# Feature-map attention with a gated MLP on one core: initial loads moved to the sync queue, normalization moved to VectorE

## The chip, the cores and the metric

The kernel runs on one NeuronCore of a Trainium2 chip. The core has a matrix engine (TensorE, PE), three engines for elementwise work (VectorE, DVE; ScalarE, ACT; GpSimd, POOL) and a sync engine (SP) that only issues DMAs. ScalarE and GpSimd can issue DMAs too. Each engine works through its own queue of instructions in order, and engines wait for each other through semaphores. The metric is the device time of one execution in microseconds; lower is better.

## The reference, cut to what matters

There are 8 batches, 8 heads, 576 tokens and a head dimension of 64. Queries and keys are projected to 128 features, and both signs are exponentiated:

```python
def phi(x):
    proj = np.einsum('bhsd,df->bhsf', x, w_phi)
    proj = proj - np.max(np.abs(proj), axis=-1, keepdims=True)
    return np.concatenate([np.exp(proj), np.exp(-proj)], axis=-1)
q_p, k_p = (phi(q), phi(k))
kv = np.einsum('bhsf,bhsd->bhfd', k_p, v)
z = np.sum(k_p, axis=2)
num = np.einsum('bhsf,bhfd->bhsd', q_p, kv)
den = np.einsum('bhsf,bhf->bhs', q_p, z)[..., None] + 1e-06
return (num / den).astype(np.float32)
```

The attention output, as rows of 512 channels, goes through a gated MLP whose gate mixes the tokens of a batch:

```python
h = np.maximum(x @ w_in, 0.0)
u, v = (h[..., :d_ff // 2].copy(), h[..., d_ff // 2:].copy())
mu = np.mean(v, axis=-1, keepdims=True)
var = np.mean((v - mu) ** 2, axis=-1, keepdims=True)
v_n = (v - mu) / np.sqrt(var + 1e-06)
v_s = np.einsum('ts,bsd->btd', w_spatial, v_n) + b_spatial[None, :, None]
gated = u * v_s
return (gated @ w_out).astype(np.float32)
```

## The kernel before

**Tiling.** A batch has 576 = 512 + 64 tokens. The 512 lie on 128 partitions with four tokens each (`main_ap`); the remaining 64, the tail, of two neighbouring batches share one tile of 128 partitions (`tail_ap`, a group g is batches 2g and 2g+1). The list `units` holds the attention work in order: a pair of heads of one batch (`pj` 0 to 3), or the shared tail of a group. Units 0 and 1 are the first two pairs of batch 0, unit 2 the tail of batches 0 and 1, units 3 and 4 the rest of batch 0, units 5 to 8 batch 1, unit 9 the next tail, and so on to 36 units.

**A unit.** `a_transpose` turns tokens and channels of k and q on TensorE (L254, VectorE or ScalarE copies the result, L256); from batch 2 on, `cross` does it with a transposing DMA. `a_keys` projects (L261), takes the largest magnitude per token and head on VectorE (L273, mk) and exponentiates on ScalarE (L276, kf). `a_scale` forms em = exp(-mk) and exp(mk) (L296) and scales v by it on GpSimd: two instructions and a small cast per pair (L301, L303, vs); for a tail `tail_scale` does so on 64 partitions (vst, shown under L61 since `pin` records it). `a_queries` takes the queries' maxima (L287), which go through TensorE and VectorE (`a_max_t`) and are subtracted inside `a_qfeat`: as extra products with `sel` up to batch 1, and from batch 2 on (`merged`) through the combined weights `wm`. `a_kv` sums kf times vs over the tokens (L373), each group of four products closed by one with the tail's vst (L375), so that a first value product needs the tail's scaling. `a_num` and `norm` divide numerator by denominator.

**The MLP of a batch.** When a batch's attention is through, `b_tasks` appends its tasks to a queue: `b_v_tail` and `b_v` (the v half of w_in, L442; ReLU on ScalarE, L444; mean and variance on VectorE, L445 and L446), `b_root`, the four normalizations `b_ln`, the u half (`b_u`, L497), the token mixing `b_s` (L518, with bias and tails in L519), and `b_o` (L543). `root` computes the reciprocal root of the variance by a power on GpSimd and from it a scale and an offset, four small GpSimd instructions (L452 to L455); `normalize` (L459) applies them on GpSimd. The tail's normalized rows go into `vnt`, whose row beside the 64 tail rows holds a one, so that the bias row of `w_spT` is added by the same product.

**Order.** `step(i)` emits the instructions of unit i in the order of `ORDER`, with lags by unit, and lets `fill` interleave MLP tasks by a credit of TensorE time. After each step the entries of `io` for that step are emitted: mostly DMA issues. An instruction wrapped in `pin` keeps its place behind the one written before it on its engine; others may be moved by the scheduler that fixes each queue when the program is built.

**Loads at the start.** SP loads two pairs of heads of batch 0's k and q as fp32 (`first`), then the bias rows (L192, L193), then batch 1's v. GpSimd issues, with the cast to bf16 in the DMA, the tails of k and q, the heads 4 and 5 of k and q, v of batch 0 in two halves, the tail of v and heads 6 and 7; among these it casts half of `first`. A pool of two buffers named v_f holds the v of two batches; k_tl, q_tl and v_tl have one buffer each.

```python
load_tail("k", 0)
load_tail("q", 0)
load("k", 0, 1, 0, 2)
load("q", 0, 1, 0, 2)
load_v(0, 0, nc.gpsimd)
```

Of the kernel before, what the change touches and what calls it, by code (L numbers as in the profile page):

```python
# [16 lines left out]
def kernel(  # L17
# [15 lines left out]
    nc = tc.nc  # L33

    B, H, S, D = q.shape
    F = w_phi.shape[1]
# [3 lines left out]
    P = 128  # L40
# [19 lines left out]
    def pin(start):  # L60
        return lambda *a, **kw: tc.keep_in_program_order(start(*a, **kw))  # L61
# [39 lines left out]
    def load_v(b, y=None, eng=nc.sync):  # L101
        if b not in st:
            alloc(b)
        h0, n = (0, H) if y is None else (4 * y, 4)
        pin(eng.dma_start)(
            out=st[b]["v"][:, h0 * NB:(h0 + n) * NB, :].rearrange("p (h c) d -> p h (c d)", h=n),
            in_=main_ap(v, b, h0, n))

    def load_tail(x, g, veng=nc.sync):
        if g not in gs:  # L110
            alloc_tail(g)
        t, eng = dict(q=(q, nc.gpsimd), k=(k, nc.gpsimd), v=(v, veng))[x]
        for i in range(2):
            pin(eng.dma_start)(out=gs[g][x][i * TL:(i + 1) * TL], in_=tail_ap(t, 2 * g + i))
# [50 lines left out]
    def fill_vnt(i, copy):  # L165
        for bl, row in ((0, TL), (1, 0)):
            pin(copy)(out=vnt[i][:, bl, :], in_=ident[:, row:row + 1].to_broadcast([P, HALF]))

    pin(nc.scalar.copy)(out=vst[0].rearrange("p b s h d -> p (b s h d)"), in_=zero.to_broadcast([P, 4 * H * DA]))
    for y in range(2):  # L170
        r = slice(y * D, (y + 1) * D)
        pin(nc.scalar.copy)(out=wphi2[r, y * F:(y + 1) * F], in_=wphi_f[r, :])
    fill_vnt(0, nc.scalar.copy)
    load_tail("k", 0)
    load_tail("q", 0)
    load("k", 0, 1, 0, 2)
    load("q", 0, 1, 0, 2)
    load_v(0, 0, nc.gpsimd)
    for x in ("k", "q"):
        pin(nc.gpsimd.tensor_copy)(out=half_tile(x, 0, 0)[:, 2:4], in_=first[x, 2])  # L180
    load_tail("v", 0, nc.gpsimd)
    load("k", 0, 1, 2, 2)
    load("q", 0, 1, 2, 2)
    load_v(0, 1, nc.gpsimd)

    w_in_bf = cpool.tile([P, KC, DFF], BF16)
    w_out_bf = cpool.tile([P, KC, DM], BF16)
    wsp = s2.tile([P, NB, T0], BF16, tag="vn", name="wsp", bufs=2)
    wspr = cpool.tile([P, NB, TL], BF16)
    wspt = s2.tile([TL, S], BF16, tag="ob", name="wspt", bufs=6)  # L190
    bsp_row = s2.tile([P, S], FP32, tag="xT", name="bsp_row", bufs=3)
    nc.sync.dma_start(out=bsp_row[TL:TL + 1, :], in_=moe_b_spatial)  # L192
# [11 lines left out]
    def transpose_spatial(i):  # L204

        pt = psum.tile([P, S], BF16, tag="bank", name="pt")
        if i < NB:
            sc = POS[i]
            for tp, c in enumerate(POS):
                nc.tensor.transpose(out=pt[:, tp * P:(tp + 1) * P], in_=wsp[:, c, bass.ds(sc, P, step=NB)],  # L210
                                    identity=ident)
            nc.tensor.transpose(out=pt[:, T0:S], in_=wspt[:, bass.ds(sc, P, step=NB)],
                                identity=ident[:TL, :TL])
            nc.vector.tensor_copy(out=w_spT[:, i, :], in_=pt)
            return
        for bl in range(2):
            lo = bl * TL
            for tp, c in enumerate(POS):
                nc.tensor.transpose(out=pt[lo:lo + TL, tp * P:(tp + 1) * P], in_=wspr[:, c, :], identity=ident)
            nc.tensor.transpose(out=pt[lo:lo + TL, T0:S], in_=wspt[:, T0:S], identity=ident[:TL, :TL])  # L220
            nc.vector.tensor_copy(out=w_spT[lo:lo + TL, NB + bl, :], in_=pt[lo:lo + TL, :])
        for bl, row in ((0, TL), (1, 0)):
            r = slice(row, row + 1)
            pin(nc.scalar.copy)(
                out=w_spT[r, NB + bl, 0:T0].rearrange("o (a b p) -> o a b p", a=2, b=2),
                in_=bsp_row[r, 0:T0].rearrange("o (p b a) -> o a b p", a=2, b=2))
            pin(nc.scalar.copy)(out=w_spT[r, NB + bl, T0:S], in_=bsp_row[r, T0:S])


    def merged(u):  # L230
        return u["pair"] and u["b"] >= XB

    def weights_with_max(n):
        for j in range(4 * n, 4 * n + 4, 2):
            pin(nc.gpsimd.tensor_copy)(out=wm[:, j, :], in_=wphi2[:, 0:F])
            pin(nc.gpsimd.tensor_tensor)(out=wm[:, j + 1, :], in0=wphi2[:, F:2 * F], in1=sel[:, j + 1, :], op=ALU.add)
            pin(nc.gpsimd.tensor_copy)(out=wm[D:D + 2 * H, j, :], in_=sel[0:2 * H, j, :])

    def q_even(u):
        u["qE"] = qts[u["i"] % len(qts)]  # L240
# [205 lines left out]
        nc.vector.bn_aggr(out=mv[r], in_=stats[r])  # L446

    def root(mv, r, n):

        var = small.tile([P, NB, 1], FP32, tag="var", name="var")  # L450
        rs = small.tile([P, NB, 2], FP32, tag="rs", name="rs")
        nc.gpsimd.tensor_scalar(out=var[r, 0:n], in0=mv[r, 0:n, 1:2], scalar1=1e-6, scalar2=None, op0=ALU.add)  # L452
        nc.gpsimd.tensor_tensor(out=rs[r, 0:n, 0:1], in0=var[r, 0:n], in1=neghalf[r, 0:n].unsqueeze(2), op=ALU.pow)
        nc.gpsimd.tensor_tensor(out=var[r, 0:n], in0=mv[r, 0:n, 0:1], in1=rs[r, 0:n, 0:1], op=ALU.mult)
        nc.gpsimd.tensor_scalar(out=rs[r, 0:n, 1:2], in0=var[r, 0:n], scalar1=-1.0, scalar2=None, op0=ALU.mult)  # L455
        return rs

    def normalize(dst, src, rs):
        nc.gpsimd.tensor_scalar(out=dst, in0=src, scalar1=rs[:, 0:1], scalar2=rs[:, 1:2],  # L459
                                op0=ALU.mult, op1=ALU.add)  # L460

    def b_v(b, j):
        d = st[b]
# [10 lines left out]

    def b_ln(b, j):
        d = st[b]
        normalize(d["vn"][:, j, :], d["vr"][j], d["rs"][:, j, :])

    def b_v_tail(g, bls):
        d = gs[g]  # L480
        r = slice(bls[0] * TL, (bls[-1] + 1) * TL)
        vr = s2.tile([P, HALF], BF16, tag="vr", name="vr", bufs=5)
        stats = small.tile([P, 6], FP32, tag="stats", name="stats")
        mv = small.tile([P, 1, 2], FP32, tag="mv_t", name="mv_t")
        v_mm(lambda kc: d["xTt"][:, kc, r], vr, r, stats, mv[:, 0, :])
        rstd = root(mv, r, 1)
        for bl in bls:
            r = slice(bl * TL, (bl + 1) * TL)
            normalize(vnt[g % 2][r, bl, :], vr[r], rstd[r, 0, :])

    def b_u(b, dc):
        d = st[b]
# [179 lines left out]
    def at(i, f, *a):  # L672
        io.setdefault(i, []).append(lambda: f(*a))

    at(0, load, "k", 1, 0)
    at(0, load, "q", 1, 0)
    at(1, fill_vnt, 1, nc.gpsimd.tensor_copy)
    at(1, load, "k", 1, 1)
    at(1, load, "q", 1, 1)
    at(1, load_v, 1)  # L680
    at(2, load_weight, w_in_bf[:, :, HALF:DFF], cols[:, :, HALF:DFF])
    at(4, load_weight, wsp, rows[:, :, 0:T0])
    at(4, load_weight, wspr, rows[:, :, T0:S])
    at(4, load_weight, wspt, moe_w_spatial[T0:S, :])
    at(5, tail_scale, 0, 1)
    at(5, load_weight, w_in_bf[:, :, 0:HALF], cols[:, :, 0:HALF])
    at(8, load_weight, w_out_bf, moe_w_out.rearrange("(kc p) f -> p kc f", p=P))
    for u in units:
        i = u["i"]
        if not u["pair"] and u["g"] > 0:  # L690
            early = 1 if u["g"] > 1 else 0
            at(i - AT - early, load_tail, "k", u["g"])
            for x in ("q", "v"):
                at(i - AT + 1 - early, load_tail, x, u["g"])
        if u["pair"] and u["b"] >= XB:
            if u["pj"] == 0:
                for n, (x, y) in enumerate((("k", 0), ("q", 0), ("k", 1), ("q", 1))):
                    at((3, 3, 5, 6)[n] if u["b"] == XB else i - AB + n, load, x, u["b"], y)
# [45 lines left out]
```

## Time and profile before

| | us |
|---|---|
| median of 8 runs | 287.27 (286.29 to 287.63) |
| the profiled execution, its own time | 287.65 |
| its span, first to last instruction | 285.7 |

| engine | busy us | share of the span | instructions |
|---|---|---|---|
| TensorE | 260.1 | 91% | 3042 |
| VectorE | 230.4 | 81% | 576 |
| ScalarE | 220.4 | 77% | 501 |
| GpSimd | 203.6 | 71% | 366 |

The profile is of one execution. Times are microseconds from the first instruction unless marked ns. A line such as L301 is a line of the kernel; what `pin` emits stands under L61. "out<-in" names the tiles, "x2" is a count. GpSimd's DMA issues count as instructions of POOL with their length, those of SP as SPq. A granted clock of 1.00 is TensorE at full speed; over the whole execution it was 0.986. TensorE's ends are modelled, so a busy TensorE is not one at its peak. Idle time is given with what released it.

### The profile page before, as it was taken

The numbers are of one execution on the slowest core, as the hardware profiler recorded it, in microseconds if no ns is written. First come the engines' busy times: TensorE is split into PE (matmuls) and PEld (weight loads), VectorE is DVE, ScalarE is ACT, GpSimd is POOL, SyncE is SP. The second block draws the span as 40 slices with busy tenths as digits, with TensorE's granted clock in tenths as the row PEclk, the third lists the DMA queues.
The fourth block names the chain that finished last, engine by engine and source line by source line (L and its number), as shares of the span: only waits on it lengthen the run. The fifth ranks groups of instructions, "written<-read, shape, count | busy, mean of one in ns | idle before, by whom it ended". The sixth has DMA issues, their size and how long they took to land.

```text
span 285.7 us, 8175 instructions
## 1 busy us (share of the span) xinstructions
PE 260.1 (91%) x3042; PEld 173.5 (61%) x3042; DVE 230.4 (81%) x576; ACT 220.4 (77%) x501; POOL 203.6 (71%) x366
## 2 busy tenths in 40 slices
PE   3861998989899999999999999999999999999993
PEld 2551876666566666666666676666766775654441
DVE  7980998986799997998889989997889897566441
ACT  6690899897699997898889997899789977723601
POOL 8669999999987895699958994789558842420710
PEclk9997799999999999999999999999999999999999
DMA  8979998999886999989988999999956201120205
GB/s 178 292 133 122 168 116 115 248 187 232 105 98 113 158 238 189 158 213 206 196 124 106 201 193 168 211 225 193 154 115 135 76 12 39 74 76 37 111 3 184
DMA packets 83420, 42.17 MB, mean 148 GB/s; under 512 B 51122, under 2 KB 78450, under 8 KB 83380
## 3 DMA queue, kind: packets, MB, share of 16 engines
q1 hardware_dynamic: 55796, 29.12, 50.3%
q0 software_dynamic: 27424, 12.46, 38.1%
q8 instruction: 24, 0.39, 0.6%
q14 instruction: 16, 0.13, 0.2%
q10 hardware_dynamic: 160, 0.07, 0.1%
HBM read 32.85 MB, written 9.44 MB: 148 GB/s over the span
## 4 chain that ended last, share of the span: by engine, by line
PE 61%; POOL 19%; DVE 6%; ACT 5%; DMA 4%; issue 3%; POOLq 0%; ACTq 0%; DVEq 0%
PE ps L518 9%; PE pv L442 9%; PE po L543 9%; PE ps L261 7%; PE pu L497 6%; PE pv L373 5%; POOL vs L301 4%; PE pn L393 4%; DMA v_f<-in_v_dram 4%; POOL vst L61 3%; PE pq L339 3%; PE ps L519 2%; DVE stats L445 2%; ACT kf L276 2%; POOL vn L459 2%
## 5 line engine op out<-in xcount | busy, mean ns | idle before, releaser
L276 ACT ACTIVATE kf<-ps 128x512 bf16<-128x512 f32 x144 | 76.2, 635 | 8.6 <-DVE mk L273 8.5
L301 POOL TENSOR_TENSOR vs<-v_f,em 128x512 bf16<-128x512 f32 x64 | 65.4, 1041 | 19.8 <-ACT em L296 14.6
L360 ACT ACTIVATE qf<-pq 128x512 bf16<-128x512 f32 x128 | 66.8, 620 | 15.6 <-PE pq L339 8.5
L273 DVE TENSOR_REDUCE mk<-ps 128x4 f32<-128x512 f32 x72 | 47.7, 677 | 0.9
L287 DVE TENSOR_REDUCE mq<-ps 128x4 f32<-128x512 f32 x62 | 39.8, 680 | 2.6 <-PE ps L261 2.2
L518 PE MATMUL ps<-w_spT,vn 128*128 128x512 bf16 x128 | 33.7, 379 | 1.4 <-POOL vn L459 1.4
L521 DVE TENSOR_TENSOR uT<-ps,uT 128x512 bf16<-128x512 f32 x32 | 22.0, 687 | 14.4 <-PE ps L519 14.4
L445 DVE BATCH_NORM_STATS2 stats<-vr 128x6 f32<-128x512 bf16 (+1 forms) x40 | 26.7, 683 | 7.3 <-ACT vr L444 6.9
L543 PE MATMUL po<-w_out_bf,uT 128*128 128x512 bf16 x128 | 32.3, 379 | 0.0
L497 PE MATMUL pu<-xT,w_in_bf 128*128 128x512 bf16 x128 | 32.1, 379 | 0.0
L442 PE MATMUL pv<-w_in_bf,xT 128*128 128x512 bf16 x128 | 31.7, 379 | 0.2
L444 ACT ACTIVATE vr<-pv 128x512 bf16<-128x512 f32 (+1 forms) x40 | 23.5, 615 | 7.5 <-PE pv L442 6.1
L373 PEld LDWEIGHTS <-kf 128*128 128x128 bf16 x512 | 22.3, 99 | 11.3 <-issue 10.4
L375 PE MATMUL pv<-vst,kf 128*128 128x66 bf16 x128 | 21.6, 193 | 7.0 <-POOL vst L61 7.0
L373 PE MATMUL pv<-vs,kf 128*128 128x66 bf16 x512 | 25.0, 195 | 2.9 <-POOL vs L303 1.6
L384 DVE TENSOR_TENSOR x<-pn,rc 128x256 bf16<-128x256 f32 x64 | 24.9, 418 | 0.3
L459 POOL TENSOR_SCALAR vn<-vr,rs 128x512 bf16<-128x512 bf16 x32 | 24.3, 767 | 1.1
L393 PEld LDWEIGHTS <-qf 128*128 128x128 bf16 x512 | 20.5, 98 | 6.8 <-issue 0.8
L499 ACT ACTIVATE uT<-pu 128x512 bf16<-128x512 f32 x32 | 19.6, 639 | 4.9 <-PE pu L497 3.2
L546 ACT COPY ob<-po 128x512 f32<-128x512 f32 x18 | 11.0, 612 | 15.1 <-PE po L543 8.6
L393 PE MATMUL pn<-kv,qf 128*128 128x66 bf16 x512 | 22.0, 195 | 0.3 <-ACT qf L360 0.3
L61 POOL TENSOR_TENSOR vst<-v_tl,em 64x512 bf16<-64x512 f32 x16 | 16.4, 1040 | 5.3 <-ACT em L296 4.9
(134 smaller groups left out, 572.5 us busy)
## 6 DMA issues: line engine op xcount, KB each, us to landing
out_dram<-ob SPq DMA_DIRECT2D x32, 256.0 KB, 2.5
v_f<-in_v_dram SPq DMA_DIRECT2D x12, 512.0 KB, 6.3
k_bf<-in_k_dram POOLq DMA_DIRECT2D x14, 256.0 KB, 6.2
q_bf<-in_q_dram POOLq DMA_DIRECT2D x14, 256.0 KB, 6.3
qt<-qT_b SPq DMA_DIRECT2D x24, 64.0 KB, 4.8
v_f<-in_v_dram SPq DMA_DIRECT2D x1, 1024.0 KB, 9.6
v_f<-in_v_dram POOLq DMA_DIRECT2D x2, 512.0 KB, 9.4
w_in_bf<-in_moe_w_in_dram POOLq DMA_DIRECT2D x2, 512.0 KB, 6.0
```

The costliest lines, as they stand in the source:

```text
L273: nc.vector.tensor_reduce(out=u["mk"][:, hs], in_=pk, axis=AX.X, op=ALU.max, apply_absolute_value=True)
L276: nc.scalar.activation(out=u["kf"][:, s, hs, :], in_=pk, func=AF.Exp, bias=0.0, scale=sc)
L287: nc.vector.tensor_reduce(out=mq[:, 4 * half:4 * half + 4], in_=pq, axis=AX.X, op=ALU.max, apply_absolute_value=True)
L301: nc.gpsimd.tensor_tensor(out=vs[:, s, :, 0:D], in0=st[u["b"]]["v"][:, pj * H:(pj + 1) * H, :], in1=em[:, s, :].unsqueeze(2).to_broadcast( ...
L360: nc.scalar.activation(out=qf[:, s], in_=pq, func=AF.Exp, bias=0.0, scale=sc)
L373: nc.tensor.matmul(out=pv[:, hh, s, :], lhsT=u["kf"][:, s, 4 * hh + c, :], rhs=u["vs"][:, s, 4 * hh + c, :], start=(c == 0), stop=False)
L393: nc.tensor.matmul(out=pn[:, pos, :], lhsT=u["qf"][hh][:, s, pos, :], rhs=d["kv"][:, 2 * u["pj"] + hh, s, :], start=(s == 0), stop=(s == 1))
L442: nc.tensor.matmul(out=pv[r], lhsT=lhs(kc), rhs=w_in_bf[:, kc, HALF:DFF], start=(kc == 0), stop=(kc == KC - 1))
L445: nc.vector.bn_stats(out=stats[r], in_=dst[r])
L497: nc.tensor.matmul(out=pu, lhsT=w_in_bf[:, kc, dc * P:(dc + 1) * P], rhs=d["xT"][:, kc, :], start=(kc == 0), stop=(kc == KC - 1))
L518: nc.tensor.matmul(out=ps, lhsT=d["vn"][:, sp, cs], rhs=w_spT[:, sp, 0:T0], start=(sp == 0), stop=False)
L543: nc.tensor.matmul(out=po[r], lhsT=lhs(dc), rhs=w_out_bf[:, dc, :], start=(dc == 0), stop=(dc == KC - 1))
```

## The change

Three things change at the start. The tails of k and q of group 0 are loaded as fp32 by SP into one tile, `tails`, that takes a v_f buffer, and GpSimd casts them; SP also loads v of batch 0 and its tail, in the order in which they are used, ahead of the bias rows. GpSimd fills both `vnt` at once, and `wm` is built at the start by two ScalarE copies and one GpSimd addition instead of twelve GpSimd instructions at steps 6 and 7. The loads of k and q of batch 1 move from steps 0 and 1 to steps 2 and 3, and the loads of weights, of batch 2 and of the next tail get steps of their own. `wspr` is no longer a tile of its own.

The bias rows are written into `w_spT` at steps 1 and 2, instead of after the transposes of the spatial weights. In the MLP, `root` keeps only the power on GpSimd, with the addition before it on VectorE, and `normalize` becomes one VectorE instruction, (v - mean) * scale.

```diff
@@ at the start
+    alloc_tail(0)
+    tails = ld.tile([P, H * NB, D], FP32, tag="v_f", name="tails")
+    for n, t in enumerate((k, q)):
+        for i in range(2):
+            pin(nc.sync.dma_start)(out=tails[i * TL:(i + 1) * TL, n * H:(n + 1) * H, :], in_=tail_ap(t, i))
+    load_v(0, 0)
+    load_tail("v", 0)
+    load_v(0, 1)
...
-    fill_vnt(0, nc.scalar.copy)
-    load_tail("k", 0)
-    load_tail("q", 0)
+    for i in range(2):
+        fill_vnt(i, nc.gpsimd.tensor_copy)
+
+    def alternate(t, i):
+        return t.rearrange("p (j two) f -> p j two f", two=2)[:, :, i, :]
+
+    pin(nc.scalar.copy)(out=alternate(wm, 0), in_=wphi2[:, 0:F].unsqueeze(1).to_broadcast([P, NP, F]))
+    pin(nc.scalar.copy)(out=alternate(wm[D:D + 2 * H], 0), in_=alternate(sel[0:2 * H], 0))
+    pin(nc.gpsimd.tensor_tensor)(out=alternate(wm, 1), in0=alternate(sel, 1),
+                                 in1=wphi2[:, F:2 * F].unsqueeze(1).to_broadcast([P, NP, F]), op=ALU.add)
+    for x in ("k", "q"):
+        pin(nc.gpsimd.tensor_copy)(out=half_tile(x, 0, 0)[:, 2:4], in_=first[x, 2])
     load("k", 0, 1, 0, 2)
     load("q", 0, 1, 0, 2)
-    load_v(0, 0, nc.gpsimd)
-    for x in ("k", "q"):
-        pin(nc.gpsimd.tensor_copy)(out=half_tile(x, 0, 0)[:, 2:4], in_=first[x, 2])
-    load_tail("v", 0, nc.gpsimd)
+    for n, x in enumerate(("k", "q")):
+        pin(nc.gpsimd.tensor_copy)(out=gs[0][x], in_=tails[:, n * H:(n + 1) * H, :])
     load("k", 0, 1, 2, 2)
     load("q", 0, 1, 2, 2)
-    load_v(0, 1, nc.gpsimd)
-    wsp = s2.tile([P, NB, T0], BF16, tag="vn", name="wsp", bufs=2)
-    wspr = cpool.tile([P, NB, TL], BF16)
+    wsp = s2.tile([P, NB, S], BF16, tag="vn", name="wsp", bufs=2)
@@ bias rows: out of transpose_spatial, the same two copies per row
+    def spatial_bias(bl):
+        r = slice(TL, TL + 1) if bl == 0 else slice(0, 1)
...
@@ def root
-        rs = small.tile([P, NB, 2], FP32, tag="rs", name="rs")
-        nc.gpsimd.tensor_scalar(out=var[r, 0:n], in0=mv[r, 0:n, 1:2], scalar1=1e-6, scalar2=None, op0=ALU.add)
-        nc.gpsimd.tensor_tensor(out=rs[r, 0:n, 0:1], in0=var[r, 0:n], in1=neghalf[r, 0:n].unsqueeze(2), op=ALU.pow)
-        nc.gpsimd.tensor_tensor(out=var[r, 0:n], in0=mv[r, 0:n, 0:1], in1=rs[r, 0:n, 0:1], op=ALU.mult)
-        nc.gpsimd.tensor_scalar(out=rs[r, 0:n, 1:2], in0=var[r, 0:n], scalar1=-1.0, scalar2=None, op0=ALU.mult)
+        rs = small.tile([P, NB, 1], FP32, tag="rs", name="rs")
+        nc.vector.tensor_scalar(out=var[r, 0:n], in0=mv[r, 0:n, 1:2], scalar1=1e-6, scalar2=None, op0=ALU.add)
+        nc.gpsimd.tensor_tensor(out=rs[r, 0:n], in0=var[r, 0:n], in1=neghalf[r, 0:n].unsqueeze(2), op=ALU.pow)
@@ def normalize
-        nc.gpsimd.tensor_scalar(out=dst, in0=src, scalar1=rs[:, 0:1], scalar2=rs[:, 1:2],
-                                op0=ALU.mult, op1=ALU.add)
+        nc.vector.tensor_scalar(out=dst, in0=src, scalar1=mv[:, 0:1], scalar2=rs, op0=ALU.subtract, op1=ALU.mult)
@@ io
-    at(0, load, "k", 1, 0)
-    at(0, load, "q", 1, 0)
-    at(1, fill_vnt, 1, nc.gpsimd.tensor_copy)
-    at(1, load, "k", 1, 1)
-    at(1, load, "q", 1, 1)
     at(1, load_v, 1)
-    at(2, load_weight, w_in_bf[:, :, HALF:DFF], cols[:, :, HALF:DFF])
+    at(1, spatial_bias, 0)
+    at(2, spatial_bias, 1)
+    at(2, load, "k", 1, 0)
+    at(2, load, "q", 1, 0)
+    at(3, load, "k", 1, 1)
+    at(3, load, "q", 1, 1)
+    at(4, load_weight, w_in_bf[:, :, HALF:DFF], cols[:, :, HALF:DFF])
+    at(4, load, "k", 2, 0)
     at(5, tail_scale, 0, 1)
     at(5, load_weight, w_in_bf[:, :, 0:HALF], cols[:, :, 0:HALF])
+    at(5, load, "q", 2, 0)
+    at(6, load_tail, "k", 1)
+    at(6, load_weight, wspt, moe_w_spatial[T0:S, :])
+    at(7, load_tail, "v", 1)
+    at(7, load_tail, "q", 1)
+    at(7, load_weight, wsp, rows)
+    at(8, load, "k", 2, 1)
+    at(8, load_v, 2, 0)
+    at(9, load, "q", 2, 1)
+    at(9, load_v, 2, 1)
+    at(9, load_weight, w_out_bf, moe_w_out.rearrange("(kc p) f -> p kc f", p=P))
...
-    at(6, weights_with_max, 0)
-    at(7, weights_with_max, 1)
```

`load_v` and `load_tail` issue on SP unless told otherwise; `alloc_tail` only takes the buffers of a tail. `weights_with_max`, which is removed, is the loop of three GpSimd instructions per pair of heads that built `wm`.

More of the change, by code (lines that the diff above doesn't have):

```diff
@@ L218, in transpose_spatial @@
             for tp, c in enumerate(POS):
-                nc.tensor.transpose(out=pt[lo:lo + TL, tp * P:(tp + 1) * P], in_=wspr[:, c, :], identity=ident)
+                nc.tensor.transpose(out=pt[lo:lo + TL, tp * P:(tp + 1) * P], in_=wsp[:, c, T0:S], identity=ident)
             nc.tensor.transpose(out=pt[lo:lo + TL, T0:S], in_=wspt[:, T0:S], identity=ident[:TL, :TL])
             nc.vector.tensor_copy(out=w_spT[lo:lo + TL, NB + bl, :], in_=pt[lo:lo + TL, :])
[L222 to L227, printed above, removed]
+    def spatial_bias(bl):
+        r = slice(TL, TL + 1) if bl == 0 else slice(0, 1)
+        pin(nc.scalar.copy)(
+            out=w_spT[r, NB + bl, 0:T0].rearrange("o (a b p) -> o a b p", a=2, b=2),
+            in_=bsp_row[r, 0:T0].rearrange("o (p b a) -> o a b p", a=2, b=2))
+        pin(nc.scalar.copy)(out=w_spT[r, NB + bl, T0:S], in_=bsp_row[r, T0:S])
     def merged(u):
         return u["pair"] and u["b"] >= XB
[L233 to L237, printed above, removed]
     def q_even(u):
@@ L450, in root, with normalize @@
         var = small.tile([P, NB, 1], FP32, tag="var", name="var")
-        rs = small.tile([P, NB, 2], FP32, tag="rs", name="rs")
-        nc.gpsimd.tensor_scalar(out=var[r, 0:n], in0=mv[r, 0:n, 1:2], scalar1=1e-6, scalar2=None, op0=ALU.add)
-        nc.gpsimd.tensor_tensor(out=rs[r, 0:n, 0:1], in0=var[r, 0:n], in1=neghalf[r, 0:n].unsqueeze(2), op=ALU.pow)
-        nc.gpsimd.tensor_tensor(out=var[r, 0:n], in0=mv[r, 0:n, 0:1], in1=rs[r, 0:n, 0:1], op=ALU.mult)
-        nc.gpsimd.tensor_scalar(out=rs[r, 0:n, 1:2], in0=var[r, 0:n], scalar1=-1.0, scalar2=None, op0=ALU.mult)
-        return rs
-    def normalize(dst, src, rs):
-        nc.gpsimd.tensor_scalar(out=dst, in0=src, scalar1=rs[:, 0:1], scalar2=rs[:, 1:2],
-                                op0=ALU.mult, op1=ALU.add)
+        rs = small.tile([P, NB, 1], FP32, tag="rs", name="rs")
+        nc.vector.tensor_scalar(out=var[r, 0:n], in0=mv[r, 0:n, 1:2], scalar1=1e-6, scalar2=None, op0=ALU.add)
+        nc.gpsimd.tensor_tensor(out=rs[r, 0:n], in0=var[r, 0:n], in1=neghalf[r, 0:n].unsqueeze(2), op=ALU.pow)
+        return rs
+    def normalize(dst, src, mv, rs):
+        nc.vector.tensor_scalar(out=dst, in0=src, scalar1=mv[:, 0:1], scalar2=rs, op0=ALU.subtract, op1=ALU.mult)
     def b_v(b, j):
@@ L476, in b_ln @@
         d = st[b]
-        normalize(d["vn"][:, j, :], d["vr"][j], d["rs"][:, j, :])
+        normalize(d["vn"][:, j, :], d["vr"][j], d["mv"][:, j, :], d["rs"][:, j, :])
     def b_v_tail(g, bls):
@@ L488, in b_v_tail @@
             r = slice(bl * TL, (bl + 1) * TL)
-            normalize(vnt[g % 2][r, bl, :], vr[r], rstd[r, 0, :])
+            normalize(vnt[g % 2][r, bl, :], vr[r], mv[r, 0, :], rstd[r, 0, :])
     def b_u(b, dc):
@@ L673, in at @@
         io.setdefault(i, []).append(lambda: f(*a))
-    at(0, load, "k", 1, 0)
-    at(0, load, "q", 1, 0)
-    at(1, fill_vnt, 1, nc.gpsimd.tensor_copy)
-    at(1, load, "k", 1, 1)
-    at(1, load, "q", 1, 1)
-    at(1, load_v, 1)
-    at(2, load_weight, w_in_bf[:, :, HALF:DFF], cols[:, :, HALF:DFF])
-    at(4, load_weight, wsp, rows[:, :, 0:T0])
-    at(4, load_weight, wspr, rows[:, :, T0:S])
-    at(4, load_weight, wspt, moe_w_spatial[T0:S, :])
+    at(1, load_v, 1)
+    at(1, spatial_bias, 0)
[6 more added lines that the diff above has]
+    at(4, load, "k", 2, 0)
     at(5, tail_scale, 0, 1)
     at(5, load_weight, w_in_bf[:, :, 0:HALF], cols[:, :, 0:HALF])
-    at(8, load_weight, w_out_bf, moe_w_out.rearrange("(kc p) f -> p kc f", p=P))
+    at(5, load, "q", 2, 0)
[9 more added lines that the diff above has]
+    at(9, load_weight, w_out_bf, moe_w_out.rearrange("(kc p) f -> p kc f", p=P))
     for u in units:
         i = u["i"]
-        if not u["pair"] and u["g"] > 0:
-            early = 1 if u["g"] > 1 else 0
-            at(i - AT - early, load_tail, "k", u["g"])
+        if not u["pair"] and u["g"] > 1:
+            at(i - AT - 1, load_tail, "k", u["g"])
             for x in ("q", "v"):
-                at(i - AT + 1 - early, load_tail, x, u["g"])
+                at(i - AT, load_tail, x, u["g"])
         if u["pair"] and u["b"] >= XB:
-            if u["pj"] == 0:
+            if u["pj"] == 0 and u["b"] > XB:
                 for n, (x, y) in enumerate((("k", 0), ("q", 0), ("k", 1), ("q", 1))):
-                    at((3, 3, 5, 6)[n] if u["b"] == XB else i - AB + n, load, x, u["b"], y)
+                    at(i - AB + n, load, x, u["b"], y)
                 for y in range(2):
```

## The prediction

> **What bounds the kernel now.** I read the chain of waits for the first 80 us first, since slice 4 of the page shows every engine but GpSimd nearly idle there. A row of the chain is start, length, and what ran or was waited for:
>
> ```profile
> 6.03 10.74 DMA v_f<-in_v_dram
> ...
> 25.43 2.25 POOL vst L61 x3
> 27.68 0.04 issue
> 27.72 0.22 PE pv L375
> ```
>
> The chain runs through GpSimd alone. It issues DMAs until 6.03, waits for batch 0's first half of v until 16.76, and ends the scaling of the shared tail's v (vst) at 27.68. Only then can TensorE do its first value product. The table of waits prices it (engine, line, what was waited for: us, times, longest):
>
> ```profile
> DVE kv L378 <- PE pv L375: 7.7, 1, 7.7
> PE pv L375 <- POOL vst L61: 7.0, 1, 7.0
> ```
>
> VectorE had finished everything else at 21.1 and stood until 28.79. What GpSimd did between the landing and vst, from its timeline:
>
> ```profile
> 16.91 2.04 POOL L301 TENSOR_TENSOR vs<-v_f,em 128x512 bf16<-128x512 f32 x2 [3.67 <-DMA v_f<-in_v_dram]
> ...
> 19.05 0.80 POOL L61 DMA_DIRECT2D k_bf<-in_k_dram  x1
> 19.84 0.76 POOL L61 DMA_DIRECT2D q_bf<-in_q_dram  x1
> ...
> 22.74 1.17 POOL L61 COPY vnt<-ident 128x512 bf16<-128x512 bf16 x2
> 23.87 0.80 POOL L61 DMA_DIRECT2D k_bf<-in_k_dram  x1
> 24.66 0.75 POOL L61 DMA_DIRECT2D q_bf<-in_q_dram  x1
> 25.43 2.05 POOL L61 TENSOR_TENSOR vst<-v_tl,em 64x512 bf16<-64x512 f32 x2
> ```
>
> Then I took the stages one by one (start:end, length, then busy us of PE, PE's weight loads, VectorE, ScalarE, GpSimd; clock, DMA share, GB/s):
>
> ```profile
> 28.70:48.00 19.30, 18.21 (x301) 15.87 (x298) 19.12 (x56) 17.62 (x43) 18.47 (x27) 0.92 0.99 128
> 48.00:75.00 27.00, 24.24 (x287) 16.63 (x287) 20.75 (x54) 23.94 (x56) 25.05 (x52) 1.00 1.21 201
> 75.00:110.00 35.00, 33.86 (x435) 23.34 (x433) 32.00 (x79) 29.76 (x70) 30.28 (x56) 1.00 1.03 154
> 110.00:140.00 30.00, 30.00 (x357) 20.14 (x355) 28.13 (x68) 27.77 (x64) 23.56 (x42) 1.00 1.17 197
> 140.00:170.00 30.00, 30.00 (x377) 20.39 (x376) 27.16 (x67) 26.70 (x65) 24.50 (x46) 1.00 1.14 149
> 170.00:230.00 60.00, 59.33 (x717) 39.53 (x715) 54.47 (x130) 52.77 (x124) 43.21 (x81) 1.00 0.96 159
> ```
>
> To 48 us VectorE is full (19.12 of 19.30), to 75 GpSimd is (25.05 of 27), and from there TensorE, with VectorE close behind: 28.13 of 30 in the tightest stretch. At the end four normalizations stand on the chain ("270.08 2.26 POOL vn L459 x3"), but TensorE idles only about a microsecond before its product at 272.4.
>
> **What the Trainium skill says.** "VectorE: DVE Perf Modes", section on the perf-mode tier table: a tensor_scalar on bf16 in SBUF may run in the 4x mode. "SBUF — State Buffer", section "Who interferes with whom": such a two-port VectorE operation and a GpSimd operation exclude one another for a whole instruction; who issues second waits. The trace agrees with both. The qt copies of L326 are also 512 bf16 elements, SBUF to SBUF; as a group of its form (busy us, mean ns) they are
>
> ```profile
> L326 DVE COPY qt<-qT_b 16x512 bf16<-16x512 bf16 x24 | 9.7, 403 | 0.8
> ```
>
> and by their line (minimum, median, maximum ns):
>
> ```profile
> L326 DVE COPY qt<-qT_b x24: 283/285/1561, 80.1 to 242.8; 16x512 bf16<-16x512 bf16 x24
> ```
>
> The longest, at 169.74, started inside two vs operations of GpSimd. "DMA: Bandwidth & Descriptors", section on queues, rings and completion order: each DMA engine consumes one queue's descriptors in ring order. No row shows that directly; it matters for the bias row below.
>
> **The change, part by part.**
>
> *Loads.* GpSimd loses eight issues at the start (k_tl 1.69, q_tl 1.40, v_tl 1.39, two v_f 0.78 each, together 6.0 us). Its wait for v hid them, so they pay only through earlier landing. On SP, v(0,0) now follows 1 MB of "first" and 512 KB of tails; the 1 MB of batch 1's v, which was issued at 3.82 ahead of it, goes behind. Between 8 and 10 us SP's queue took 55 ns for a 1 KB packet on 16 engines; between 46 and 48 us 31 ns for a 256 B one. So: first full-rate data at 2.4 us (the same view from 0 to 4), 1024 packets of 1 KB 3.5, 2048 of 256 B 4.0, v's 512 of 1 KB 1.8, and 0.6 to completion (q's first load, due at 4.16 by this count, is cast at 4.76): v(0,0) at 12.3 against 16.76, v's tail (1024 of 256 B, 2.0) at 14.3.
>
> *GpSimd's start.* Four vnt fills at 0.6 end at 3.9. The wm addition needs ScalarE's wphi2 (5.7 before) and perhaps its two wm copies (about 0.6 each): 1.04, as a 512-element L301, or 1.7 as four of today's; it ends at 6.8 to 8.1. Two casts 1.22, two issues 1.5, two tail casts 1.22, two issues 1.5: free at 12.3 to 13.5. The casts of k and q tail end at 11.4 and 12.0 at the latest, where TensorE transposes the tail at 11.2 and 12.3 today: no loss.
>
> *To the first product.* vs of unit 0 (2.04 plus 0.2) from 13.5 to 15.75, unit 1 (em at 13.3 today) to 18.0, vst (its em at 16.7) 18.0 to 20.25. Four issues (3.1) and the vnt fill (1.17) no longer stand between. Before: 27.7. **Gain 7.5**; VectorE's 7.66 of waiting caps it, so what is late next is VectorE itself, full from there to 48.0.
>
> *Bias row.* Four ScalarE copies (2.53 us at 60.9) go to steps 1 and 2, 1.27 each, into the 1.15 us in which ScalarE waits for VectorE today: nothing, if the row is there. Its DMA now stands behind v(0,1) on SP, so it lands at 2.4+3.5+4.0+1.8+2.0+1.8+0.6 = 16.1, while ScalarE's turn may come at 13.3. Queued behind it: unit 2's kf and em, for which vst waits. If it stalls: kf from 17.4 instead of 14.5, em at 19.9, vst at 22.2 instead of 20.25, and 2 us of the 7.5 are gone; ScalarE's backlog (kf and qf of three units at about 2.1 each) I put at 1 more. Order among operations that are not pinned is set when the program is built, so I can't tell; I take no stall.
>
> *Batch 1's v* needs a v_f buffer of two, which batch 0 and the tails hold. If it gets the tails' (free at 12) it lands about 20. If it must wait for batch 0's (last read at about 27.8) it lands at 34, and its vs, due at 30.0, comes 4 late, 2.7 of it beyond GpSimd's lead over today's schedule.
>
> *Weights, w_in, wsp.* wm's twelve small operations (4.1 us at 49.6 to 56.5) and the wspr issue (0.75) leave GpSimd. w_in's half is issued near 28, as now, long before its first use.
>
> *Normalization.* Per batch GpSimd loses five at 0.767 and three small ones for each of two roots (0.24, 0.19, 0.25): 5.2 us. VectorE gains five at 0.40 (bounds: 0.285 alone; 0.68 like bn_stats if no fast mode) and two additions at 0.15 (0.10 like the sel1 addition, 0.17 like L446): **2.3 us**. A fetch from GpSimd's power (1.05 and 0.58) now lies between two VectorE operations.
>
> *48 to 75 us.* GpSimd sheds 4.1+0.75+1.5+0.7+3.0 = 10.0 of 25.05; ScalarE's bias copies leave 21.4 of 23.94; VectorE rises to 23.0. TensorE's 24.24 is then fullest. At most 27.0-24.24 = 2.8; I take **2.5** (bounds 0 and 4, since modelled matmul ends hide waits).
>
> *75 to 258 us.* VectorE idles 1.9, 2.8 and 2.8 us per 30; 2.3 more nearly fill it. TensorE stays first, but with no reserve on VectorE. I charge 0.3 a batch for six batches, less 0.3 for GpSimd's earlier vs: **loss 1.5** (bounds: gain 1, loss 7).
>
> *End.* TensorE's wait before 272.4 goes: **gain 1.0** (0.5 to 1.5).
>
> Sum: -7.5-2.5+1.5-1.0 = -9.5, against the profiled execution's 287.65 us (span 285.7 and about 2.0 around it): 278.15. The median of the runs is 0.38 lower, so the forecast is **277.8 us**.
>
> **Rivals.** (1) The bias row holds ScalarE: 277.8+3 = 280.8. For: its loads are last in line on SP. Against: kf and em of unit 2 are not pinned and may be put ahead. (2) Batch 1's v waits for batch 0's buffer: 280.5. (3) Slower: VectorE becomes the bound from batch 1 on, because its queue holds addition, GpSimd's power and normalization directly one behind another (the list of tasks puts root and first normalization together at cost 0.0), and everything behind them stands. Price: powers 1.05+0.58 and four hand-overs at 0.1 are 2.0 a batch, and half the time a vs pair (2.04) stands ahead of the power: 3.0. VectorE's 2.5 of idle already goes to the 2.3, so 6.5 batches lose about 2.0 to 3.0 each over the 1.5 counted: 277.8+12 = 290. It decides from some 1.5 us lost per batch. Against: today's GpSimd timeline has a DMA issue between normalizations, so the built order does mix in other work. (4) The normalizations cost 0.285 each, with GpSimd emptier, and VectorE's rest absorbs them: 277.8-1.5-1.5 (the 4 instead of 2.5) = 274.8, down to 272.5.
>
> **How the numbers follow.** As forecast 0.50 (its own range 275.5 to 280); bias row 0.25; buffer 0.07; slower 0.10; hidden entirely 0.08. The range 272.5 to 284 leaves out the slower case and little else. Faster by over 0.2% 0.90, within 0.2% (0.6 us, about what this kernel's runs can tell) 0.02, slower 0.08: the slower case, less its near end.
>
> **What would show it.** Right: vst ends near 20, VectorE's wait for L375 falls below 1 us, vs of unit 0 starts near 13.5, and normalizations on VectorE take 0.3 to 0.4. Wrong: a ScalarE wait on the bias row's DMA near 13 to 17; a GpSimd wait for batch 1's v near 30; VectorE idle on GpSimd's power; VectorE above 29.5 of 30 with TensorE below 29 after 110 us.

## The result and the profile after

The changed kernel is slower: a median of 301.63 us (300.24 to 304.0, 11 runs) against 287.18 us (285.92 to 288.27, 31 runs) of the kernel before in the same series. The ratio is 1.050, with a 95% interval of 1.048 to 1.052. Runs more than 1.5% above the fastest of the same kernel count in no ratio and in no median below, while the recorded expectations use medians of all runs, which are up to 1.3 us higher. The profiled execution took 300.57 us, its span 298.8 us, and TensorE was busy for 89% of it (before: 91%).

The start went nearly as planned. From GpSimd's timeline after (start, length, instruction, idle before it and its releaser):

```profile
13.03 2.04 POOL L310 TENSOR_TENSOR vs<-v_f,em 128x512 bf16<-128x512 f32 x2
...
18.85 2.03 POOL L61 TENSOR_TENSOR vst<-v_tl,em 64x512 bf16<-64x512 f32 x2 [1.48 <-ACT em L305]
```

The scaling of unit 0's v starts at 13.03 instead of 16.91, the tail's vst ends at 21.08 instead of 27.68, and the first kv copy ends at 22.3 instead of 29.2, 6.9 us earlier. VectorE's wait of 7.7 us for the first value product is gone.

What took its place is in the table of waits of the changed kernel (engine, line, what was waited for: us in total, times, longest):

```profile
POOL rs L461 <- DVE var L460: 29.5, 7, 16.4
DVE vnt L465 <- POOL rs L461: 11.1, 5, 4.0
DVE vn L465 <- POOL rs L461: 6.0, 8, 1.2
ACT w_spT L61 <- DMA bsp_row<-in_moe_b_spatial_dram: 2.3, 1, 2.3
```

VectorE stands 17.1 us in 13 waits before its normalizations, for the power on GpSimd. It had no such wait before. ScalarE stands 2.3 us for the bias row. Now the same stretches as in the prediction (start:end, length, then busy us of PE, PE's weight loads, VectorE, ScalarE, GpSimd; clock, DMA share, GB/s):

```profile
28.70:48.00 19.30, 18.14 (x282) 14.12 (x280) 18.47 (x51) 18.25 (x45) 18.61 (x32) 1.00 1.15 143
48.00:75.00 27.00, 24.10 (x291) 16.85 (x290) 22.42 (x61) 18.87 (x45) 19.50 (x31) 1.00 1.12 183
75.00:110.00 35.00, 32.64 (x387) 21.37 (x386) 32.08 (x79) 29.12 (x69) 20.29 (x35) 1.00 1.32 192
110.00:140.00 30.00, 25.85 (x309) 17.10 (x307) 25.05 (x67) 23.48 (x55) 16.59 (x29) 1.00 0.98 155
140.00:170.00 30.00, 28.19 (x316) 18.08 (x314) 27.02 (x63) 25.26 (x59) 17.87 (x30) 1.00 1.00 155
170.00:230.00 60.00, 54.82 (x649) 36.69 (x648) 51.72 (x130) 47.00 (x110) 28.72 (x51) 0.97 0.86 144
```

In the stretch from 110 to 140 us, where VectorE was given more work, it is busy 25.05 us, against 28.13 before, and TensorE falls from 30.00 to 25.85. No engine is full. The time goes into waits between engines.

One such wait can be followed through the chain that ended last (start, length, what ran):

```profile
120.87 2.26 POOL vst L61 x3
...
123.18 0.19 POOL mhl L299
...
123.45 0.20 POOL mhl L300
123.64 0.54 POOL rs L461
124.19 0.03 issue
124.21 0.40 DVE vnt L465
...
126.62 0.59 DVE mk L282
127.20 0.02 issue
127.23 1.09 ACT kf L285 x2
```

and through VectorE's own timeline in the same stretch:

```profile
120.24 0.15 DVE L460 TENSOR_SCALAR var<-mv_t 64x1 f32<-64x1 f32 x1
120.31 0.40 DVE L393 TENSOR_TENSOR x<-pn,rc 128x256 bf16<-128x256 f32 x1
124.21 0.40 DVE L465 TENSOR_SCALAR vnt<-vr,mv_t,rs 64x512 bf16<-64x512 bf16 x1 [3.50 <-POOL rs L461]
```

VectorE makes the addition at 120.24, does one more instruction, and then stands for 3.50 us at the tail's normalization (vnt). GpSimd needs 0.57 us for the power, but first works off what is ahead in its queue: the scaling of the next tail (vst), 4.6 us from 118.57 on, and two small steps on the queries' maxima (mhl). Behind VectorE's waiting normalization stand the next mk, and behind mk the exponentials: ScalarE idles 3.21 us until 127.23.

A simple measure of the pace is the start of the first token-mixing product of each batch, read from the timelines of TensorE, and its distance to the one of the next batch:

| us between batches | 0-1 | 1-2 | 2-3 | 3-4 | 4-5 | 5-6 | 6-7 |
|---|---|---|---|---|---|---|---|
| before | 34.9 | 29.9 | 29.1 | 30.7 | 29.8 | 26.1 | 17.4 |
| after | 36.5 | 34.8 | 32.3 | 35.2 | 32.5 | 26.1 | 17.5 |

The kernel after starts this row 2.9 us ahead (69.9 against 72.8) and loses 17.0 us on the way, all but 0.1 of it while attention work of later batches is mixed in. Behind the row it gets 1.1 us back: from the first token-mixing product of batch 7 to the end it takes 13.9 us, before 15.0.

### The profile page after: what moved, and what is told of

It is laid out like the page before. It is cut to its first block, busy times and chain, and to the rows that moved or that the text cites. A ratio compares the mean times of both kernels' runs of the same rounds, so it can differ in the third digit from the quotient of the medians.

```text
span 298.8 us, 8079 instructions
## 1 busy us (share of the span) xinstructions
PE 265.0 (89%) x3042; PEld 173.9 (58%) x3042; DVE 248.1 (83%) x632; ACT 222.0 (74%) x501; POOL 155.8 (52%) x262
## 4 chain that ended last, share of the span: by engine, by line
PE 48%; DVE 17%; POOL 16%; ACT 5%; issue 5%; DMA 5%; SPq 3%; POOLq 0%; ACTq 0%; DVEq 0%
PE ps L523 9%; PE po L548 7%; PE pv L451 6%; PE pu L502 5%; POOL vst L61 5%; POOL vs L310 5%; DVE mk L282 4%; DVE mq L296 4%; PE ps L270 4%; ACT kf L285 3%; PE pv L382 3%; SPq L61 3%; POOL rs L461 2%; PE pq L348 2%; PE ps L524 2%
## 5 line engine op out<-in xcount | busy, mean ns | idle before, releaser
L461 POOL TENSOR_TENSOR rs<-var,neghalf 64x1 f32<-64x1 f32 (+1 forms) x16 | 12.7, 796 | 40.9 <-DVE var L460 29.5
L523 PE MATMUL ps<-w_spT,vn 128*128 128x512 bf16 x128 | 32.9, 380 | 0.0
L548 PE MATMUL po<-w_out_bf,uT 128*128 128x512 bf16 x128 | 32.7, 381 | 0.1
```

Of the source, the lines that this page charges most:

```text
L523: nc.tensor.matmul(out=ps, lhsT=d["vn"][:, sp, cs], rhs=w_spT[:, sp, 0:T0], start=(sp == 0), stop=False)
L548: nc.tensor.matmul(out=po[r], lhsT=lhs(dc), rhs=w_out_bf[:, dc, :], start=(dc == 0), stop=(dc == KC - 1))
```

## The experiments

The theories: **A**, VectorE's queue stands for the power, which is late because GpSimd's queue is worked off in order too. **B**, VectorE has too much work. **C**, the start's gain is given back, because the loads of later batches were moved behind. **D**, GpSimd's queue stands at the power for VectorE's addition, and the scalings behind the power come late. Medians are given with their ratio to the kernel before in the same series, whose median was between 286.97 and 287.36 us.

**1. The loads alone.** The changed kernel with the old root and normalization on GpSimd.

```diff
-        nc.vector.tensor_scalar(out=var[r, 0:n], in0=mv[r, 0:n, 1:2], scalar1=1e-6, scalar2=None, op0=ALU.add)
+        nc.gpsimd.tensor_scalar(out=var[r, 0:n], in0=mv[r, 0:n, 1:2], scalar1=1e-6, scalar2=None, op0=ALU.add)
...
-        nc.vector.tensor_scalar(out=dst, in0=src, scalar1=mv[:, 0:1], scalar2=rs, op0=ALU.subtract, op1=ALU.mult)
+        nc.gpsimd.tensor_scalar(out=dst, in0=src, scalar1=rs[:, 0:1], scalar2=rs[:, 1:2],
+                                op0=ALU.mult, op1=ALU.add)
```

> The changed kernel with the old root and the old normalization on GpSimd (four small instructions and one per row tile), everything else as changed. Theory A (the fetch: VectorE's queue stands for GpSimd's power): the loss is all in the normalization, so 278 to 281 us. Theory B (VectorE is simply too full with five more instructions per batch): the same, 278 to 281. Theory C (the new order of loads and constants costs the later batches): 295 to 301.

Measured: 284.88 us, ratio 0.992 (0.989 to 0.995), which lies between the two ranges expected. The trace is of an execution of 288.94 us, in which ScalarE stands 4.3 us for the bias row and the first kv copy ends 4.9 us earlier than before. From batch 0 to batch 1 the distance is 38.6 us (before 34.9); from there the pace is that of before (30.0, 29.1, 30.6, 29.8, 26.1, 17.4). So the loss of the later batches comes with the normalization. But the loads bring only 2.1 us (286.97 - 284.88), far less than the first kv copy comes early.

**2. The normalization alone.** The kernel before with the changed root and normalize.

> The kernel before with the new root and normalization alone. Theories A and B: 287 plus what the steady batches lost in the changed kernel (18.5 us between the first products of batch 0 and batch 6), so 300 to 306 us. Theory C: 286 to 289.

Measured: 308.44 us, ratio 1.073 (1.070 to 1.077): 21 us of loss from this part alone, somewhat more than expected. The row starts 3.9 us later than before (76.7 against 72.8), so some of the loss lies ahead of it. Its distances between batches are those of the changed kernel (36.6, 34.8, 32.3, 35.1, 32.5, 26.1, 17.4), and VectorE waits for the power here too, 19.4 us in 13 waits:

```profile
DVE vnt L456 <- POOL rs L452: 13.1, 5, 4.8
DVE uT L517 <- PE ps L515: 7.8, 13, 1.3
DVE kv L378 <- PE pv L375: 7.7, 1, 7.7
DVE vn L456 <- POOL rs L452: 6.3, 8, 1.2
```

**3. No power.** The changed kernel with all its VectorE work; the addition writes the scale directly, and the power is left out, so that the rows are scaled by the variance and not by its reciprocal root.

```diff
-        nc.vector.tensor_scalar(out=var[r, 0:n], in0=mv[r, 0:n, 1:2], scalar1=1e-6, scalar2=None, op0=ALU.add)
-        nc.gpsimd.tensor_tensor(out=rs[r, 0:n], in0=var[r, 0:n], in1=neghalf[r, 0:n].unsqueeze(2), op=ALU.pow)
+        nc.vector.tensor_scalar(out=rs[r, 0:n], in0=mv[r, 0:n, 1:2], scalar1=1e-6, scalar2=None, op0=ALU.add)
```

> The changed kernel without the power: VectorE's addition writes the scale directly, so the reciprocal root is left out of the computation and nothing goes to GpSimd between the addition and the normalization; VectorE keeps the same number of instructions. Theory A: the waits of VectorE for the power (17.1 us in 13 waits) go, 278 to 283 us. Theory B: VectorE is as full as before, 294 to 301.

Measured: 287.35 us, ratio 1.002 (0.9995 to 1.005). The fetch of the power costs 14.3 us (301.63 - 287.35). What VectorE's normalizations cost without the fetch is about the distance to the loads alone, 287.35 - 284.88 = 2.5 us. This missed the 278 to 283 us that theory A expected, by what theory C explains below; theory B's 294 to 301 us is far.

**4. The power computed twice.** The first goes into a tile that nobody reads.

```diff
+        once = small.tile([P, NB, 1], FP32, tag="once", name="once")
+        pin(nc.gpsimd.tensor_tensor)(out=once[r, 0:n], in0=var[r, 0:n], in1=neghalf[r, 0:n].unsqueeze(2), op=ALU.pow)
-        nc.gpsimd.tensor_tensor(out=rs[r, 0:n], in0=var[r, 0:n], in1=neghalf[r, 0:n].unsqueeze(2), op=ALU.pow)
+        pin(nc.gpsimd.tensor_tensor)(out=rs[r, 0:n], in0=var[r, 0:n], in1=neghalf[r, 0:n].unsqueeze(2), op=ALU.pow)
```

> The changed kernel with the power computed twice on GpSimd, one directly behind the other, the first into a tile that nobody reads; VectorE's work and its order stay. GpSimd gets 0.57 plus 1.05 us a batch, 13 us in all, of which it has 143 us idle. Theory A (VectorE stands for the power, so what is added to the power is added to the path in each batch with attention behind it, some six of them): 308 to 313 us. Theory B (VectorE's own load decides): 301 to 304 us.

Measured: 312.77 us, ratio 1.088 (1.084 to 1.092), 11.1 us over the changed kernel, for 13 us put on an engine that is busy 52% of the changed kernel's span. VectorE's waits:

```profile
DVE vn L467 <- POOL rs L61: 17.2, 8, 3.4
DVE vnt L467 <- POOL rs L61: 15.3, 8, 4.5
```

These are 32.5 us against 17.1. More delay of the power is more time of the kernel, as theory A expected.

**5. Normalizations written later.** On VectorE as in the change, but as tasks after the second to fourth task of the u half, and pinned there. In the trace (an execution of 291.63 us) 12 to 32 VectorE instructions stand between an addition and the first normalization that needs it, in all batches but the last, instead of at most 2 in 15 of 16 cases; that is more than the 5 to 15 planned.

```diff
...
-            normalize(vnt[g % 2][r, bl, :], vr[r], mv[r, 0, :], rstd[r, 0, :])
+            d["ln", bl] = (vnt[g % 2][r, bl, :], vr[r], mv[r, 0, :], rstd[r, 0, :])
...
         for y in range(NB):
-            ts += ns[y:y + 1] + outs[2 + y:3 + y] + us[y:y + 1]
+            ts += outs[2 + y:3 + y] + us[y:y + 1]
+            if y == 1:
+                ts.append((0.0, lambda: b_ln_tail(g, bl)))
+            if y > 1:
+                ts += ns[2 * y - 4:2 * y - 2]
```

> The changed kernel with its normalizations on VectorE, as it has them, but written later and kept in that order: the tail's after the second product task of the u half, the four others after the third and the fourth, so that 5 to 15 other VectorE instructions stand between the addition and the first normalization that needs GpSimd's power. Theory A (VectorE's queue stands for the power, which costs about 14 us): 286 to 290 us, with the waits of the normalizations on the power below 3 us in all. Theory B (it is the load of the normalizations on VectorE, wherever they stand): 298 to 303 us.

Measured: 289.59 us, ratio 1.008 (1.005 to 1.010). The runs spread widely, from 287.08 to 294.27 us, and the median of all 20 is 290.92. The order alone gives back 12.0 of the 14.3 us (10.7 with all runs), with the same work on the same engines. VectorE's waits for the power have left the table, while GpSimd stands for the addition as long as it did:

```profile
POOL rs L461 <- DVE var L460: 30.5, 8, 16.3
```

In the changed kernel that was 29.5 us in 7 waits, so theory D falls: this wait stays and the time comes back. Instead TensorE now waits for the later rows:

```profile
PEld L526 <- DVE vn L61: 6.0, 11, 1.4
...
PE ps L526 <- DVE vn L61: 3.0, 4, 0.9
```

**6. GpSimd normalizes in the changed form.** Only the engine of the new normalize is changed; the addition stays on VectorE.

```diff
-        nc.vector.tensor_scalar(out=dst, in0=src, scalar1=mv[:, 0:1], scalar2=rs, op0=ALU.subtract, op1=ALU.mult)
+        nc.gpsimd.tensor_scalar(out=dst, in0=src, scalar1=mv[:, 0:1], scalar2=rs, op0=ALU.subtract, op1=ALU.mult)
```

> The changed kernel with its new root (addition on VectorE, power on GpSimd), but the normalization on GpSimd. VectorE gives its sum away and does not wait for it; GpSimd waits for VectorE's addition. Theory A: 279 to 284 us. Theory B: 278 to 282. A third theory D, that GpSimd standing at the power for VectorE's addition (29.5 us in 7 waits in the changed kernel) is what delays the keys' scaling behind it: 290 to 300.

Measured: 323.34 us, ratio 1.126 (1.119 to 1.132), outside every expectation, and it says nothing on the theories, because of a size that I had not known. The instructions of its normalize line on GpSimd (minimum, median, maximum ns, first and last start):

```profile
L465 POOL TENSOR_SCALAR vn<-vr,mv,rs x32: 2062/2076/2207, 64.9 to 310.6; 128x512 bf16<-128x512 bf16 x32
```

and of the old form, from the kernel with the loads alone:

```profile
L468 POOL TENSOR_SCALAR vn<-vr,rs x32: 760/772/797, 65.3 to 273.0; 128x512 bf16<-128x512 bf16 x32
```

(v - mean) * scale takes GpSimd 2.08 us, v * scale + offset 0.77 us, on the same tile: 40 times 1.3 us are 52 us more. The tails take as long as the rows in both kernels. TensorE then waits for the rows, 32.7 us in its weight loads alone.

**7. The bias row later.** The loads alone (experiment 1), with the bias row at steps 5 and 6.

```diff
-    at(1, spatial_bias, 0)
-    at(2, spatial_bias, 1)
+    at(5, spatial_bias, 0)
+    at(6, spatial_bias, 1)
```

> The changed kernel with the old root and normalization on GpSimd, as before (285.3 us, 2.3 us of gain where the start alone brings the first kv copy 6.9 us forward), and the bias row written into w_spT at steps 5 and 6 instead of 1 and 2. Theory C1 (the start's gain is partly lost because ScalarE stands 2.3 to 4.3 us for the bias row's DMA): 281.5 to 283.5 us. Theory C2 (that wait only moves time, since batch 2's loads, transposes and the weights come two to three steps later and are what is waited for at 50 to 85 us): 284.5 to 286 us.

Measured: 286.29 us, ratio 0.996 (0.994 to 0.998). ScalarE's wait for the row is gone and nothing is won: the time is 1.4 us above experiment 1. Until the third kv copy the lead is 6.5 us, and at the ninth it is 2.4 us (80.4 against 82.8). Between them VectorE stands for a copy of batch 2's transposed queries:

```profile
76.74 0.41 DVE L334 COPY qT_b<-pt 16x512 bf16<-16x512 bf16 x1 [4.57 <-DMA qt<-qT_b]
```

That copy waits for a small DMA out of the tile, this one follows a transposing DMA (issued at 66.91), and that one the load of the second half of batch 2's q, which GpSimd issues here at

```profile
62.56 0.88 POOL L61 DMA_DIRECT2D q_bf<-in_q_dram  x1
```

The load is one of step 9. It came 11.4 us after the DMA before it in the queue, and behind the two tail scalings and the normalization that stand between. The kernel before issues it at 48.81, from step 6.

**8. The later loads at their old steps.** As 7, with batch 2's k, q and v, the next tail and the weights at the steps of the kernel before.

```diff
-    at(4, load, "k", 2, 0)
-    at(5, load, "q", 2, 0)
-    at(8, load, "k", 2, 1)
-    at(9, load, "q", 2, 1)
-    at(7, load_weight, wsp, rows)
+    at(3, load, "k", 2, 0)
+    at(3, load, "q", 2, 0)
+    at(5, load, "k", 2, 1)
+    at(6, load, "q", 2, 1)
+    at(4, load_weight, wsp, rows)
...
```

> As the kernel with the late bias row, and the loads of batch 2, of the next tail and of the weights issued at the steps of the kernel before (batch 2's k and q at steps 3, 5 and 6, spatial weights at 4, next tail at 4 and 5, w_in at 2 and 5, w_out at 8); the start and the loads of batch 1 stay as changed. Theory C2 (the late loads give the start's gain back): 278.5 to 281.5 us, and no wait of a microsecond or more on the spatial weights or on batch 2's transposed queries. Theory C3 (VectorE, full to 48 us, takes the start's gain back whatever is loaded when): 284 to 286 us.

Measured: 282.31 us, ratio 0.983 (0.979 to 0.987). The same load is issued at

```profile
43.94 0.81 POOL L61 DMA_DIRECT2D q_bf<-in_q_dram  x1
```

and the ninth kv copy keeps 5.8 of the 6.6 us that the first one is ahead. So 4.0 us (286.29 - 282.31) of the start's gain had been given back by loads and weights that were moved up to three steps back, and theory C3 falls. All of them were moved together, so the share of the one load followed above is not shown. The time is 0.8 us above what C2 expected.

**9. The bias row at its old place too**, after the transposes of the spatial weights.

```diff
+        for bl in range(2):
+            spatial_bias(bl)
...
-    at(5, spatial_bias, 0)
-    at(6, spatial_bias, 1)
```

> As the kernel with the earlier loads (282.3 us; old normalization on GpSimd, changed start, batch 2's loads, tail and weights at the steps of before), with the bias row written where the kernel before writes it, after the transposes of the spatial weights. In the kernel with the bias row at steps 5 and 6 the fifth kv copy (index 4) falls 2.2 us behind the pace of the first four. Theory C4 (ScalarE's 2.5 us for the bias row cost as much on the path anywhere among the first six units): 280 to 281 us. Rival (between the kv copies they only fill a gap that the batches after make up): 282 to 283 us.

Measured: 280.56 us, ratio 0.977 (0.974 to 0.981), the fastest version here, 6.8 us under the kernel before. The median fits C4, but the intervals of this and of 8 overlap, and the two profiled spans are 279.5 and 279.6 us, with the ninth kv copy at 76.9 and 77.0. Whether the place of the bias row is worth anything stays open. In this kernel the stages after 75 us look as they did before the change:

```profile
75.00:110.00 35.00, 33.91 (x445) 23.55 (x443) 32.30 (x78) 31.55 (x76) 26.93 (x50) 1.00 1.31 180
110.00:140.00 30.00, 30.00 (x348) 19.69 (x346) 27.34 (x66) 26.85 (x63) 25.13 (x44) 1.00 1.19 186
140.00:170.00 30.00, 29.83 (x392) 20.51 (x390) 27.76 (x68) 26.32 (x64) 24.09 (x44) 1.00 1.17 179
```

**10. Experiment 5 with the loads and bias row of 9.**

> The kernel with VectorE's normalizations written later (290.9 us), with the loads and the bias row of the kernel above. If the two causes are independent (late loads 4.0 us, as measured without VectorE's normalization): 285.5 to 287.5 us. If the lateness of the loads is hidden behind VectorE's normalizations: 290 to 291.5 us.

Measured: 288.43 us, ratio 1.004 (1.003 to 1.006), between the two expectations: loads and bias row give 1.2 us here (2.5 with all runs of experiment 5), and 4.3 us where GpSimd normalizes (experiment 1 to 9). Even with the wait covered, the kernel is 7.9 us behind kernel 9. Of these some 2.5 us are the normalizations without the fetch, by experiment 3. TensorE's weight loads wait 5.8 us in 10 waits for the later rows in this kernel; that this is the rest was not tried apart.

## Why the prediction was wrong

The forecast was 277.8 us, the time 301.63, so 23.8 us are to be found. The runs give them as a ladder: the fetch of the power 14.3 (changed kernel to experiment 3), the normalizations without the fetch 2.5 (to 1), the later loads with the bias row's place 4.3 (1 to 9), and 2.8 for what kernel 9, which normalizes on GpSimd, still lacks to the forecast. The steps of the ladder are not independent: with VectorE's normalizations (5 to 10) the loads and the bias row were worth 1.2, not 4.3.

**Start, -7.5: right in place and nearly in size.** Scaling from 13.03 (forecast 13.5), vst done at 21.08 (20.25), the first kv copy 6.9 us earlier. In kernel 9, where the first kv copy is 6.1 us early, the gain reaches the end: -6.8.

**Bias row, no stall: wrong, but no cost of it was shown.** Rival 1's wait came: ScalarE stood until 15.22 (it named 16.1), and GpSimd 1.48 us for unit 2's em. But moving the row alone won nothing.

**Batch 1's v: right.** GpSimd's waits have none for v.

**48 to 75 us, -2.5: wrong.** TensorE is busy 24.10 of 27 us, as little as before (24.24), though GpSimd is down from 25.05 to 19.50, by 5.6 of the 10.0 us counted. The lead of 5.4 us at the fifth kv copy has become 4.1 at the ninth. The failed step is one that the sum doesn't have: batch 2's k and q were moved from steps 3 to 6 to steps 4 to 9 and the spatial weights from step 4 to steps 6 and 7, and I priced only what GpSimd shed, not what arrived later. Experiments 7 and 8 price it at 4.0 us without VectorE's normalizations. Its share in the changed kernel is not shown, for there the first wait for the power falls into the same stretch:

```profile
52.64 0.40 DVE L465 TENSOR_SCALAR vnt<-vr,mv_t,rs 64x512 bf16<-64x512 bf16 x1 [2.77 <-POOL rs L461]
```

**Durations on VectorE: about right.** The normalizations take 0.41 us in the median, forecast 0.40. From the groups by form (busy us, mean ns):

```profile
L465 DVE TENSOR_SCALAR vn<-vr,mv,rs 128x512 bf16<-128x512 bf16 x32 | 16.2, 526 | 6.0 <-POOL rs L461 6.0
L465 DVE TENSOR_SCALAR vnt<-vr,mv_t,rs 64x512 bf16<-64x512 bf16 x8 | 3.3, 410 | 11.2 <-POOL rs L461 11.1
L460 DVE TENSOR_SCALAR var<-mv 128x4 f32<-128x4 f32 x8 | 2.1, 267 | 0.1
L460 DVE TENSOR_SCALAR var<-mv_t 64x1 f32<-64x1 f32 x8 | 1.2, 145 | 0.1
```

That is 22.8 us in all, 2.85 per batch against 2.3. The mean of 526 ns comes mostly from four that took 1.18 to 1.28 us; each of them overlaps two scalings by GpSimd of about 1.03 us, as here:

```profile
165.02 1.25 DVE L465 TENSOR_SCALAR vn<-vr,mv,rs 128x512 bf16<-128x512 bf16 x1 [0.57 <-POOL rs L461]
165.08 2.09 POOL L310 TENSOR_TENSOR vs<-v_f,em 128x512 bf16<-128x512 f32 x2
```

The Trainium skill, "SBUF — State Buffer", section "Who interferes with whom", says that such a two-port operation and a GpSimd operation exclude one another for the whole instruction. The trace fits: six normalizations overlap a scaling, these four among them, and each ends 0.15 us after a scaling ends.

**75 to 258 us, +1.5: wrong, the main error.** The pace shows 17.0 us of loss. The load I had counted about right; the failed step is the fetch, which I noted ("now lies between two VectorE operations") and then charged at nothing. It cost 14.3 us by experiment 3. It is rival 3, held at 0.10 and priced at 290: right in its mechanism, and too low in its price. It counted the powers, four hand-overs and half a vs pair, 3.0 us a batch, of which some was to be covered; its 290 is moreover the low end of its own sum, which at 3.0 a batch for 6.5 batches, less the 1.5 counted, gives 295.8. In the case shown, two tail scalings and the maxima stood ahead of the power and the wait was 3.50 us for the tail's row alone. My argument against it, that the built order mixes in other work, read the order of GpSimd's queue, where normalization stood before; on VectorE at most two instructions stood between addition and normalization in 15 of 16 cases.

**End, -1.0: right.** The last batch's first four products on normalized rows stood twice for GpSimd before, and now run through:

```profile
270.72 0.60 PE L518 MATMUL ps<-w_spT,vn 128*128 128x512 bf16 x2
271.64 0.39 PE L518 MATMUL ps<-w_spT,vn 128*128 128x512 bf16 x1 [0.32 <-POOL vn L459]
272.39 0.39 PE L518 MATMUL ps<-w_spT,vn 128*128 128x512 bf16 x1 [0.36 <-POOL vn L459]
...
284.87 1.03 PE L523 MATMUL ps<-w_spT,vn 128*128 128x512 bf16 x4
```

The product behind them starts 1.89 us after the first (272.61), now 0.86 us (285.73). That is the 1.0 us forecast, and it is most of the 1.1 us that the table of paces leaves for the end.

The statement of what would show it wrong, VectorE idle on GpSimd's power, holds. The other, VectorE above 29.5 of 30, doesn't: it is at 25.05.

## What to carry to other kernels

When one small step of a computation stays on another engine, price the round trip and not the step: what stands ahead of it in that engine's queue, and what stands behind the waiting instruction on the first. A busy share falls when such waits appear, so an engine with room is no comfort. Move all of a chain or none, or put independent work between request and use (here this was worth 12.0 us, or 10.7 over all runs). And when loads are moved back to let others go first, follow each to its first reader: in experiment 7 the lead fell from 6.5 to 2.4 us where VectorE stood 4.6 us behind a load that was issued 14 us later.

## What the runs showed that I had not expected

On GpSimd the two forms of the same normalization differ by a factor of 2.7: 2.08 us for subtract and multiply against 0.77 us for multiply and add, both with two scalars per partition on 128x512 bf16. On VectorE subtract and multiply took 0.41 us. Which of the operations makes the difference on GpSimd was not tried apart.

The bias row shows how late a transfer of 2 KB can be that comes last on a queue: issued at 9.50, landed at 15.2.
